# A kernel's own scheduler: dates for the next pair's x operands, and a smaller margin for pressing work

## The chip, the cores and the metric

One core of one Trainium2 chip runs the whole program: TensorE (PE), VectorE (DVE), ScalarE (ACT), GpSimd (POOL) and SyncE (SP), which issues nearly all transfers. The metric is the device time of one execution in microseconds (us). Before the change the median of three runs is 1017.37 us (1017.28 to 1018.18).

## The reference

Attention with a sigmoid in place of the softmax, and then two MLPs one behind the other, all in float32:

```python
scores = scale * np.matmul(q, k.transpose(0, 1, 3, 2)) - np.log(S)     # (4, 12, 448, 448)
attn = 1.0 / (1.0 + np.exp(-scores))
x = np.matmul(attn, v)                     # heads side by side: (1792, 768)
h = x @ w_in;  r = np.maximum(h, 0.0)      # first MLP, 768 -> 2048 -> 768
x = (r * r) @ w_out
h = x @ w_in2                              # second MLP, same sizes
out = (np.maximum(h, 0.0) + alpha * np.minimum(h, 0.0)) @ w_out2
```

The weights arrive as float64.

## The kernel before, in words

Every float32 product is made from a rounded "high" part and the rest, the "low" part: three matmuls (high by high, high by low, low by high) in place of one. ACT makes high parts (an activation that copies into the rounded type), DVE or POOL make low parts (a subtraction). The inner products of the MLPs are also made by a scheme of seven block products from sums and differences of blocks (Strassen's kind), so an x operand or a weight operand is often a sum of blocks before it is split.

The attention comes first (about 159 us, written out in a fixed order, untouched here). After it come 32 units of work, `UNITS` in line 164: layer (2) by pair of batches (2) by eight blocks of two 128-wide slices of the hidden width. Eight units of one layer and one pair are called a phase: phase 0 is layer 0, pair 0; phase 1 is layer 0, pair 1; phase 2 is layer 1, pair 0; phase 3 is layer 1, pair 1. A unit n belongs to phase n // 8. In phases 0 and 2 each unit does its inner products (line 555) and its outer products (line 578), and its weights are made on the spot: a load of 64-bit words into the buffer `raw` (lines 197 to 205), two ACT passes (`scale`, lines 216 and 218), a DVE pass that joins the words (line 231), sums (lines 252 to 258), and the split (lines 269 and 273). The buffer `raw` has two halves, and the load of the next unit's inner weights takes both, so it waits until the outer weights in it have been joined. In phases 1 and 3 the weights come back from DRAM (lines 714 and 890), and the outer products are made for two units at a time (`out_block`, lines 872 to 1031, matmuls in line 942, sums in line 905, splits in lines 919 to 934).

Inside a unit the result of an inner product leaves its PSUM bank by an ACT copy (line 762) or a DVE addition (line 766), then goes through the nonlinearity (lines 732 to 748) and a split (lines 736 and 749) to the outer products; their results are added up by DVE (lines 840 and 973).

**The x operands of the next pair.** While one phase runs, the x operands for the next phase are prepared: `add_x_sum` (line 641) adds a difference of two blocks (line 295), `add_waiting` (line 1039) adds an ACT copy into the one buffer `stage` (line 299), a subtraction into its other half (line 302) and a store of `stage` to DRAM by SP (line 1043). In phase 1 the blocks are loaded in pieces from DRAM (`add_pieces`, line 1048). POOL does differences and subtractions in phases 0 and 1, DVE in phase 2 (`X_BY`, line 1036). Lines 1085 to 1100 hand these steps out to units: four to a unit in phases 0 and 2, from the second unit on, five to a unit in phase 1. At the end of a phase the stored operands are loaded into the x buffers (line 1107). There is one `stage`, so a step's copy waits for the store of the step before it.

**What sets the order.** From line 609 on nothing is issued at once: `Plan.add` records every step with its engine, a cost in us and what it reads and writes. `Plan.run` (lines 50 to 127) then plays the whole list through and issues the steps in the order of the times that come out. TensorE's steps keep their order; each has a due time, the sum of PE costs before it. Any other step is due so early that what needs it can be in time (line 65); `due` is the latest start. In `choose` an engine takes, of the steps that are ready, the one due first, whatever unit it was added in, and it leaves a step aside if a step due earlier would become ready before that one ends and its end would come later than that due time less `MARGIN` (line 96). A step that is not left aside runs as soon as its engine is free, however far off its due time is. The order on each engine, SP's queue of transfers among them, is then fixed when the program runs.

Of the kernel before, what the change touches and what calls it, by code (L numbers as in the profile page):

```python
# [9 lines left out]
F32 = mybir.dt.float32  # L10
# [9 lines left out]
class Plan:  # L20
# [5 lines left out]


    HOP = 0.10
    MARGIN = 2.5
    DEPTH = 3.0  # L30
    AFTER_OWN = {"ACT": 0.12, "POOL": 0.05}
    TAIL = {"PE": 0.17, "DVE": 0.085, "ACT": 0.095, "POOL": 0.04}

    def __init__(self):
        self.jobs, self.last, self.readers = [], {}, {}

    def add(self, engine, us, emit, reads=(), writes=(), port=False, size=0):
        reads, writes = set(reads), set(writes)
        before = {self.last[k] for k in reads | writes if k in self.last}
        for k in writes:  # L40
            before |= self.readers.pop(k, set())
        me = len(self.jobs)
        before.discard(me)
        self.jobs.append((engine, us, emit, before, port, size))
        for k in writes:
            self.last[k] = me
        for k in reads:
            self.readers.setdefault(k, set()).add(me)

    def run(self):  # L50
        jobs, n = self.jobs, len(self.jobs)
        after = [[] for _ in jobs]
        for j, job in enumerate(jobs):
            for i in job[3]:
                after[i].append(j)

        def length(j):
            return jobs[j][1] if jobs[j][0] != "SP" else jobs[j][5] + 2.0

        at, due, pe = 0.0, [0.0] * n, [j for j in range(n) if jobs[j][0] == "PE"]  # L60
        for j in pe:
            due[j] = at
            at += jobs[j][1]
        for j in reversed(range(n)):
            late = min((due[s] - self.HOP for s in after[j]), default=at + 50.0) - length(j) - self.TAIL.get(jobs[j][0], 0.0)
            due[j] = min(due[j], late) if jobs[j][0] == "PE" else late
        left = [len(job[3]) for job in jobs]
        ready = [0.0] * n
        engines = ("PE", "DVE", "ACT", "POOL", "SP", "NIL")
        free = dict.fromkeys(engines, 0.0)  # L70
        waiting = {e: [] for e in engines}
        next_pe = 0
        port_free = dma_free = 0.0
        for j in range(n):
            if not left[j]:
                waiting[jobs[j][0]].append(j)
        order = []

        def begin(j, t):
            t = max(t, ready[j])  # L80
            if jobs[j][0] == "SP":
                t = max(t, dma_free - self.DEPTH)
            return max(t, port_free) if jobs[j][4] else t

        def choose(e, give_way=True):
            queue = waiting[e]
            if e == "PE":
                queue = [j for j in queue if j == pe[next_pe]]
            if not queue:
                return None  # L90
            t = max(free[e], min(begin(j, free[e]) for j in queue))
            now = sorted((j for j in queue if begin(j, free[e]) <= t + 1e-9), key=lambda j: due[j])
            soon = [j for j in queue if begin(j, free[e]) > t + 1e-9]
            for j in now:
                end = t + jobs[j][1]
                if any(due[s] < due[j] and begin(s, free[e]) < end and end > due[s] - self.MARGIN for s in soon):
                    continue
                if e == "POOL" and give_way and any(jobs[s][4] and due[s] < min(due[j], end) and max(free["DVE"], ready[s]) < end for s in waiting["DVE"]):
                    continue
                return t, j  # L100
            if not soon:
                return None
            s = min(soon, key=lambda j: begin(j, free[e]))
            return begin(s, free[e]), s

        while len(order) < n:
            t, j, e = min([(*c, e) for e in engines if (c := choose(e))] or [(*c, e) for e in engines if (c := choose(e, False))])
            engine, us, emit, before, port, size = jobs[j]
            waiting[e].remove(j)
            if e == "PE":  # L110
                next_pe += 1
            free[e] = t + us
            end = t + us + self.TAIL.get(e, 0.0)
            if port:
                port_free = t + us
            if e == "SP" or size:
                dma_free = max(dma_free, t + 0.1) + size
                end = dma_free + 2.0
            order.append((t, j))
            for s in after[j]:  # L120
                left[s] -= 1
                ready[s] = max(ready[s], t + us + self.AFTER_OWN.get(e, 0.0) if jobs[s][0] == e and e != "SP" else end + self.HOP)
                if not left[s]:
                    waiting[jobs[s][0]].append(s)
        self.span = free["PE"]
        for t, j in sorted(order):
            jobs[j][2]()
# [3 lines left out]
def fused_kernel(ctx: ExitStack, tc: tile.TileContext, q, k, v, w1i, w1o, w2i, w2o, alpha, out):  # L131
# [15 lines left out]
    nc = tc.nc  # L147
    B, H, S, D = q.shape
# [144 lines left out]
    def x_sum(p, i, c, eng):  # L293
        to, x, y = (x_block(p, name, c) for name in X_SUM[i])
        eng.tensor_sub(to, x, y)  # L295
# [11 lines left out]
    with tc.manual_schedule():  # L307
# [6 lines left out]
        with tc.tile_pool(name="apool", bufs=1) as apool, tc.tile_pool(name="apsum", bufs=1, space=bass.MemoryType.PSUM) as psum:  # L314
# [145 lines left out]
            for what in X_ORDER[:-1]:  # L460
                i = int(what[1])
# [6 lines left out]
            for d in range(ND):  # L468
                u, w = 2 * d, 2 * d + 1
                i = d - 4  # L470
# [64 lines left out]
        stage = mpool.tile([P, 2, S], F32R, name="stage")  # L535
# [73 lines left out]
        plan = Plan()  # L609
        add = plan.add  # L610
# [11 lines left out]
        def dve(cols):  # L622
            return 0.07 + 0.00105 * cols

        def pool(cols):
            return 0.13 + 0.0023 * cols

        PE_IN, PE_OUT = 0.2027, {384: 0.1740, 512: 0.2270}
        BYTES = 4 * P

        def moved(size, run):

            return size / run * (0.037 + run / 30e3) / 16

        def cells_of(p, name, c):
            kh, t = PLACE[name]
            if p is None:
                return old_cells(PIECES + (kh * 2 + t) * S, S)
            return [("acc", p, ((kh * KH + c) * 2 + t) * S // CELL + k) for k in range(S // CELL)]

        def add_x_sum(p, i, c, engine):
            to, x, y = X_SUM[i]
            add(engine, pool(S) if engine == "POOL" else dve(S), lambda: x_sum(p, i, c, nc.gpsimd if engine == "POOL" else nc.vector), cells_of(p, x, c) + cells_of(p, y, c), cells_of(p, to, c), port=True)

        def add_x_parts(p, i, c, engine, where, keys):
            hi, lo = where
# [71 lines left out]
        def old_cells(at, size):  # L718
            return [("acc", 0, k) for k in range(at // CELL, -(-(at + size) // CELL))]
# [316 lines left out]
        X_BY = ("POOL", "POOL", "DVE")  # L1036
        x_kept = {}

        def add_waiting(n, i, c, p, engine):
            keys = [("stage", 0), ("stage", 1)]  # L1040
            add_x_parts(p, i, c, engine, (stage[:, 0], stage[:, 1]), keys)
            to = x_kept[n // NB]
            add("SP", 0.05, lambda: nc.sync.dma_start(out=to[i][:, :, c], in_=stage.bitcast(F32)), keys, [("x_kept", i, c)], size=moved(2 * S * BYTES, 4 * S))

        def add_pieces(c):

# [3 lines left out]
        for n in range(NU):  # L1050
            layer, p, fp = UNITS[n]
            other, phase = 1 - p, n // NB
            by_pieces = phase == 1
# [31 lines left out]
            if phase < 3:  # L1085
                if fp == 0:
                    x_kept[phase] = [dpool.tile([P, 2, KH, S], F32, name=f"kept_x{n}_{i}") for i in range(7 if by_pieces else 4)]
                    if by_pieces:
                        steps = [(what, c) for c in range(KH) for what in ("load", *X_ORDER) if c < KH - 1 or what not in ("p3", "p4", "p5", "p6")]
                    else:  # L1090
                        steps = [None] * 4 + [(what, c) for what in X_WAITING if what != "p3" or layer == 0 for c in range(KH)]
                if fp < NB - 1:
                    each = 5 if by_pieces else 4
                    for what, c in filter(None, steps[each * fp:each * fp + each]):
                        if what == "load":
                            add_pieces(c)
                        elif what[0] == "s":
                            add_x_sum(None if by_pieces else other, int(what[1]), c, X_BY[phase])
                        else:
                            add_waiting(n, int(what[1]), c, None if by_pieces else other, X_BY[phase])  # L1100
            outward = add_outward(n) if p == 0 else None
# [8 lines left out]
            if p == 0:  # L1110
                next(outward, None)
            elif fp % 2:
                next(part_way, None)
            else:
                part_way = out_block(n + 1)
                next(part_way)
        plan.run()


# [28 lines left out]
```

## Time and profile before

| | us |
|---|---|
| median of the runs (three) | 1017.37 |
| the profiled execution | 1018.92 |
| its span | 1017.1 |
| PE busy | 1008.2 (99%) |
| DVE busy | 730.2 (72%) |
| ACT busy | 636.6 (63%) |
| POOL busy | 281.0 (28%) |

The span is the profiled execution from its first to its last instruction. TensorE's granted clock is 1.00 in all stretches. "Busy" of PE contains matmuls that run into each other; idle time of the other engines costs only where PE waits. The rows further down come from the page's list of engines, from tables by stretch (time, busy time and instructions of each engine, granted clock, DMA share, GB/s), from lists of instructions in order of time (start, duration, engine, line, operation, result and inputs, count; in brackets idle time before it and what ended it), and from the chain of work that ended last.

### The profile page before, as it was taken

The numbers are of one execution on the slowest core, as the hardware profiler recorded it, in microseconds if no ns is written. First come the engines' busy times: TensorE is split into PE (matmuls) and PEld (weight loads), VectorE is DVE, ScalarE is ACT, GpSimd is POOL, SyncE is SP. The second block draws the span as 40 slices with busy tenths as digits, with TensorE's granted clock in tenths as the row PEclk, the third lists the DMA queues.
The fourth block names the chain that finished last, engine by engine and source line by source line (L and its number), as shares of the span: only waits on it lengthen the run. The fifth ranks groups of instructions, "written<-read, shape, count | busy, mean of one in ns | idle before, by whom it ended". The sixth has DMA issues, their size and how long they took to land.

```text
span 1017.1 us, 15048 instructions
## 1 busy us (share of the span) xinstructions
PE 1008.2 (99%) x5539; PEld 886.6 (87%) x5539; DVE 730.2 (72%) x968; ACT 636.6 (63%) x976; POOL 281.0 (28%) x240
## 2 busy tenths in 40 slices
PE   9999999999999999999999999999999999999998
PEld 6555557988998899998899999999999999999998
DVE  5556886367777774868786885888888776676857
ACT  4566777767776655776566667666666565535352
POOL 0001222346321130435342511111111227070703
PEclk9999999999999999999999999999999999999999
DMA  6566747677776699698768966766666983626133
GB/s 145 148 175 166 201 118 291 268 285 281 280 279 231 246 418 364 224 335 292 279 247 330 372 240 217 251 251 245 217 229 234 391 282 83 198 80 201 45 95 109
DMA packets 133337, 237.59 MB, mean 234 GB/s; under 512 B 56976, under 2 KB 81552, under 8 KB 131856
## 3 DMA queue, kind: packets, MB, share of 16 engines
q1 hardware_dynamic: 130384, 234.79, 67.3%
q10 hardware_dynamic: 2880, 1.84, 0.6%
q8 instruction: 44, 0.72, 0.3%
q14 instruction: 29, 0.24, 0.1%
HBM read 150.74 MB, written 85.85 MB: 233 GB/s over the span
## 4 chain that ended last, share of the span: by engine, by line
PE 90%; DVE 4%; DMA 2%; issue 2%; POOL 1%; ACT 1%; SPq 0%; DVEq 0%; POOLq 0%; ACTq 0%
PE h L555 38%; PE o L578 20%; PE o L942 11%; PE h L942 7%; PE av L408 5%; PE sc L388 4%; PE h L578 1%; DMA raw<-in_moe_w_in_dram 1%; PE scr L398 1%; PE tp L355 1%; PE av L416 1%; DMA words<-kept5o 1%; PE tp L358 1%; DVE flat L361 1%; PE busy L432 0%
## 5 line engine op out<-in xcount | busy, mean ns | idle before, releaser
L555 PE MATMUL h<-x,wi 128*128 128x448 f32 (+1 forms) x2064 | 416.4, 361 | 1.6 <-DVE c L766 1.6
L555 PEld LDWEIGHTS h<-x,wi 128*128 128x128 f32 x2064 | 379.6, 188 | 31.7 <-DVE c L766 2.0
L700 POOL TENSOR_TENSOR wo<-words,wo 128x384 fp32r<-128x384 f32 x64 | 69.3, 1107 | 242.9 <-ACT wo L703 238.8
L578 PE MATMUL o<-g,wo 128*128 128x512 f32 (+1 forms) x528 | 112.9, 367 | 1.0 <-DVE acc L840 0.8
L578 PE MATMUL o<-wo,g 128*128 128x384 f32 x624 | 112.4, 335 | 0.0
L578 PEld LDWEIGHTS o<-wo,g 128*128 128x128 f32 x624 | 109.1, 188 | 0.4
L578 PEld LDWEIGHTS o<-g,wo 128*128 128x128 f32 x528 | 96.0, 188 | 14.2 <-DVE acc L840 2.4
L840 DVE TENSOR_TENSOR acc<-o,acc 128x768 f32<-128x768 f32 (+2 forms) x91 | 85.6, 950 | 12.9 <-PE o L578 12.7
L766 DVE TENSOR_TENSOR c<-h,c 128x448 f32<-128x448 f32 x72 | 44.6, 622 | 69.2 <-PE h L555 66.9
L390 ACT ACTIVATE a<-sc,bias 128x896 f32<-128x896 f32 x72 | 69.1, 1004 | 35.6 <-PE av L408 22.6
L924 POOL TENSOR_TENSOR wo<-acc,wo 128x384 fp32r<-128x384 f32 x30 | 35.7, 1209 | 137.2 <-ACT wo L919 137.2
L216 ACT ACTIVATE raw<-raw 128x768 f32<-128x768 f32 x64 | 58.2, 909 | 23.3 <-DMA raw<-in_moe_w_out_dram 19.3
L762 ACT ACTIVATE c<-h 128x448 f32<-128x448 f32 x72 | 38.7, 539 | 43.9 <-PE h L555 43.8
L749 DVE TENSOR_TENSOR g<-c,g 128x448 fp32r<-128x448 f32 x64 | 43.4, 681 | 31.6 <-ACT c L737 21.5
L302 POOL TENSOR_TENSOR stage<-acc,stage 128x448 fp32r<-128x448 f32 x29 | 35.9, 1237 | 99.2 <-ACT stage L299 99.2
L231 DVE SCALAR_TENSOR_TENSOR words<-raw 128x768 int32<-128x768 int32 x53 | 52.8, 1005 | 9.7 <-ACT raw L218 8.9
L408 PE MATMUL av<-a,v 128*64 128x448 f32 x288 | 59.4, 548 | 0.0
L218 ACT ACTIVATE raw<-raw 128x768 int32<-128x768 uint32 x64 | 57.7, 902 | 0.0
L973 DVE TENSOR_TENSOR acc<-o,acc 128x384 f32<-128x384 f32 (+1 forms) x84 | 46.1, 580 | 14.7 <-PE o L942 14.4
L295 POOL TENSOR_TENSOR acc<-acc 128x448 f32<-128x448 f32 x28 | 40.6, 1451 | 27.9 <-DMA acc<-late 16.2
L745 DVE SCALAR_TENSOR_TENSOR c<-c,nal,pos 128x448 f32<-128x448 f32 x48 | 34.5, 718 | 17.0 <-ACT c L744 15.9
L408 PEld LDWEIGHTS av<-a,v 128*64 128x64 f32 x288 | 18.5, 136 | 28.7 <-issue 26.8
(168 smaller groups left out, 1691.2 us busy)
## 6 DMA issues: line engine op xcount, KB each, us to landing
wi<-kept_w SPq DMA_DIRECT2D x112, 384.0 KB, 5.2
kept_w<-wi SPq DMA_DIRECT2D x45, 768.0 KB, 4.3
raw<-in_moe_w_out_dram SPq DMA_DIRECT2D x32, 768.0 KB, 4.8
raw<-in_moe_w_in_dram SPq DMA_DIRECT2D x13, 1536.0 KB, 8.9
kept_x<-stage SPq DMA_DIRECT2D x38, 448.0 KB, 5.8
x<-kept_x SPq DMA_DIRECT2D x10, 1344.0 KB, 11.0
kept_w<-wi SPq DMA_DIRECT2D x22, 384.0 KB, 4.9
v<-in_v_dram SPq DMA_DIRECT2D x24, 192.0 KB, 2.9
```

What stands on the lines that cost most here:

```text
L216: nc.scalar.activation(half.bitcast(F32), half.bitcast(F32), AF.Prelu, scale=2.0 ** -112, alpha=2.0 ** 32)
L218: nc.scalar.activation(half, half.bitcast(U32), AF.Copy, scale=2.0 ** -29 * (1 - 2.0 ** -12), bias=-0.5 + 7.5 * 2.0 ** -12)
L231: nc.vector.scalar_tensor_tensor(out=to, in0=raw_words(at, 1, both), scalar=3, in1=raw_words(at, 0, both), op0=ALU.logical_shift_left, op1 ...
L390: nc.scalar.activation(sig[u, j], ps[:, :, :S], AF.Sigmoid, bias=bias[:, :1], scale=SCALE)
L408: nc.tensor.matmul(avs[u][h * D:(h + 1) * D, :S], vals[u][:, h, j, :], a[:, h, :], start=(u % 2 == 0 and j == 0), stop=(u % 2 == 1 and j = ...
L555: nc.tensor.matmul(ps[:, a:e], W[:, OPERAND[k], wp, c * P:(c + 1) * P], X[k][:, xp, c, a:e], start=(k in OPENING and c == 0 and i == 0 and ...
L578: nc.tensor.matmul(ps, *ops, start=(begin and i == 0), stop=(end and i == len(ways) - 1), skip_group_check=True)
L700: nc.gpsimd.tensor_sub(WO[j][:, 1, at], words["o"][:, j, at], WO[j][:, 0, at])
L766: add("DVE", dve(S), lambda: nc.vector.tensor_add(to, hb[b][:, :S], to), [("h", b), *key], key)
L840: add("DVE", dve(count), lambda dst=dst, src=src: nc.vector.tensor_add(dst, src, dst), [*src_keys, *cells], cells)
L942: nc.tensor.matmul(ps[:, a:e], stationary(ways, j), moving(ways, j)[:, a:e], start=(start and j == 0 and i == 0 and a == 0), stop=(j == 1 ...
L973: add("DVE", dve(out_wide), lambda: nc.vector.tensor_add(part, src, part), [key, *cells], cells)
```

## The change

`MARGIN` goes from 2.5 to 1.0. `Plan` gets a list of the places where units end (`step`), and a step may be given `by`, a unit's number. Where a step has one, its due time is at most the due time of the first PE step that was added after that unit, less the step's own length; steps that it depends on are dated back from there as before. The x differences, and the stores of `stage`, that are handed out in unit n get `by` = n + 2. Costs, instructions and their dependencies are as before; only the order of issue can differ.

```diff
-    MARGIN = 2.5
+    MARGIN = 1.0
...
-    def add(self, engine, us, emit, reads=(), writes=(), port=False, size=0):
+        self.steps, self.by = [], {}
+    def step(self):
+        self.steps.append(len(self.jobs))
+    def add(self, engine, us, emit, reads=(), writes=(), port=False, size=0, by=None):
...
+        if by is not None:
+            self.by[me] = by
...
             due[j] = min(due[j], late) if jobs[j][0] == "PE" else late
+            if j in self.by and self.by[j] < len(self.steps):
+                due[j] = min(due[j], next((due[i] for i in pe if i >= self.steps[self.by[j]]), at) - length(j))
...
-        def add_x_sum(p, i, c, engine):
+        def add_x_sum(p, i, c, engine, by):
...
-            add(engine, pool(S) if engine == "POOL" else dve(S), lambda: x_sum(p, i, c, nc.gpsimd if engine == "POOL" else nc.vector), cells_of(p, x, c) + cells_of(p, y, c), cells_of(p, to, c), port=True)
+            add(engine, pool(S) if engine == "POOL" else dve(S), lambda: x_sum(p, i, c, nc.gpsimd if engine == "POOL" else nc.vector), cells_of(p, x, c) + cells_of(p, y, c), cells_of(p, to, c), port=True, by=by)
...
-            add("SP", 0.05, lambda: nc.sync.dma_start(out=to[i][:, :, c], in_=stage.bitcast(F32)), keys, [("x_kept", i, c)], size=moved(2 * S * BYTES, 4 * S))
+            add("SP", 0.05, lambda: nc.sync.dma_start(out=to[i][:, :, c], in_=stage.bitcast(F32)), keys, [("x_kept", i, c)], size=moved(2 * S * BYTES, 4 * S), by=n + 2)
...
-                            add_x_sum(None if by_pieces else other, int(what[1]), c, X_BY[phase])
+                            add_x_sum(None if by_pieces else other, int(what[1]), c, X_BY[phase], n + 2)
...
                 next(part_way)
+            plan.step()
         plan.run()
...

```

## Rows read from the trace of the kernel before

**Rows 1.** The page's list of engines: busy us, share of the span, instructions.
```profile
PE 1008.2 (99%) x5539; PEld 886.6 (87%) x5539; DVE 730.2 (72%) x968; ACT 636.6 (63%) x976; POOL 281.0 (28%) x240
```

**Rows 2.** Stretches: us; PE, PEld, DVE, ACT, POOL busy (instructions); clock, DMA share, GB/s.
```profile
158.94:379.78 220.84, 219.81 (x1098) 199.33 (x1097) 151.53 (x196) 152.37 (x244) 69.36 (x59) 1.00 0.79 292
213.85:241.97 28.12, 27.86 (x138) 24.81 (x137) 18.94 (x24) 17.39 (x29) 16.10 (x14) 1.00 0.68 232
269.26:296.54 27.28, 27.28 (x138) 24.95 (x137) 20.30 (x27) 19.99 (x32) 7.77 (x7) 1.00 0.80 289
296.54:324.90 28.36, 27.59 (x138) 24.87 (x137) 19.66 (x27) 18.44 (x29) 3.99 (x4) 1.00 0.71 252
...
379.78:587.97 208.19, 206.18 (x1046) 190.33 (x1044) 153.09 (x184) 134.11 (x208) 77.12 (x62) 1.00 0.85 307
...
483.20:536.67 53.47, 51.84 (x263) 47.45 (x261) 41.08 (x50) 30.99 (x49) 22.02 (x18) 1.00 0.72 259
536.67:587.97 51.30, 51.30 (x263) 47.66 (x261) 40.23 (x53) 34.43 (x53) 17.90 (x15) 1.00 0.95 360
587.97:807.15 219.18, 219.18 (x1193) 212.04 (x1192) 178.68 (x258) 141.89 (x230) 38.86 (x35) 1.00 0.68 248
```

**Rows 3.** Instructions in order of time, sixth unit of phase 0.
```profile
299.46 0.90 ACT L218 ACTIVATE raw<-raw 128x768 int32<-128x768 uint32 x1
...
302.30 0.62 DVE L766 TENSOR_TENSOR c<-h,c 128x448 f32<-128x448 f32 x1 [1.60 <-PE h L555]
302.84 1.56 DVE L231 SCALAR_TENSOR_TENSOR words<-raw 128x768 int32<-128x768 int32 x1
...
304.49 0.38 SPq L205 DMA_DIRECT2D raw<-in_moe_w_in_dram  x1
...
305.10 0.62 DVE L749 TENSOR_TENSOR g<-c,g 128x448 fp32r<-128x448 f32 x1 [0.69 <-ACT c L737]
...
307.31 2.15 PEld L578 LDWEIGHTS o<-g,wo 128*128 128x128 f32 x12
```

**Rows 4.** The chain that ended last, same unit: start, us, what.
```profile
304.49 10.74 DMA raw<-in_moe_w_in_dram
```

**Rows 5.** Instructions in order of time, third unit of phase 0.
```profile
226.03 0.62 DVE L749 TENSOR_TENSOR g<-c,g 128x448 fp32r<-128x448 f32 x1 [0.40 <-ACT c L737]
...
230.29 2.99 POOL L295 TENSOR_TENSOR acc<-acc 128x448 f32<-128x448 f32 x2
...
230.89 1.37 DVE L273 TENSOR_TENSOR wi<-words,wi 128x768 fp32r<-128x768 f32 x1
...
232.18 2.12 DVE L749 TENSOR_TENSOR g<-c,g 128x448 fp32r<-128x448 f32 x2
```

**Rows 6.** Instructions in order of time, third unit of phase 2.
```profile
642.76 11.12 PE L555 MATMUL h<-x,wi 128*128 128x224 f32 x55
...
649.28 0.62 DVE L766 TENSOR_TENSOR c<-h,c 128x448 f32<-128x448 f32 x1
...
652.48 0.63 DVE L749 TENSOR_TENSOR g<-c,g 128x448 fp32r<-128x448 f32 x1
...
653.52 2.15 PEld L578 LDWEIGHTS o<-wo,g 128*128 128x128 f32 x12
```

**Rows 7.** Instructions in order of time, phase 1, around its longest PE wait.
```profile
473.89 0.60 SPq L1043 DMA_DIRECT2D kept_x<-stage  x1
...
494.16 0.95 DVE L231 SCALAR_TENSOR_TENSOR raw<-raw 128x768 int32<-128x768 int32 x1
```

**Rows 8.** The chain that ended last, same stretch: start, us, what.
```profile
475.25 8.09 DMA words<-kept5o
```

**Rows 9.** The store of `stage` in phase 0, and in phase 1: durations, first and last start.
```profile
L1043 SPq DMA_DIRECT2D kept_x<-stage x12: 518/519/1059, 185.3 to 292.9; - x12
...
L1043 SPq DMA_DIRECT2D kept_x<-stage x17: 513/519/604, 425.1 to 571.7; - x17
```

**Rows 10.** Waits in phase 1: us in total, times, longest.
```profile
ACT stage L299 <- DMA kept_x<-stage: 14.9, 7, 4.2
```

## What is forecast, and from which rows

> **What bounds the kernel now.** I read the page's list of engines first: PE is busy 1008.2 of 1017.1 us [rows 1], so nothing but PE's own work and the short waits in it sets the end. Then the table by stretch, where the reader is to compare length and PE busy time [rows 2]. Phase 2 has no gap at all: 219.18 of 219.18. An undisturbed unit of phase 0 takes 27.28 (269.26 to 296.54), so phase 0's 220.84 holds 220.84 - 8 x 27.28 = 2.60 of delay; two units have most of it, 28.12 (0.84 over) and 28.36 (1.08 over). An undisturbed pair of units of phase 1 takes 51.30 (536.67 to 587.97), so phase 1's 208.19 holds 208.19 - 4 x 51.30 = 2.99, of which the pair from 483.20 has 53.47 - 51.30 = 2.17. An order of issue adds or removes no PE work, so 2.60 + 2.99 = 5.6 us is all that it can win (0.55% of the time). Third, the lists in order of time and the chain, for what stands behind each delay.
>
> **The smaller margin.** It removes no instruction. It lets DVE, ACT and POOL begin a filler step (a join, a scale, a sum) beside a pressing one that would become ready before it ends, as long as 1.0 us, not 2.5, is left to the pressing one's latest start.
>
> *The sixth unit of phase 0 (1.08).* ACT ends the last scale at 299.46 + 0.90 = 300.36, and the join that needs it could run on DVE then. DVE stands idle for 1.60 us, does the pressing addition at 302.30 and only then the join, at 302.84 [rows 3]. The load of the next inner weights needs that join and is issued at 304.49; it lands 10.74 us later and is at the head of the chain that delays PE [rows 3, 4]. How much room had the addition? Its chain to the split takes 305.10 + 0.62 - 302.30 = 3.42, PE loads the result as weights at 307.31 [rows 3], so its latest start is 307.31 - 3.42 = 303.89, 1.59 after it could start. A margin of 2.5 is more than that room, so no filler may overlap its start at all; a margin of 1.0 leaves 0.59 for overlap. The join alone takes 0.95 (a twin, [rows 7]) and on the real times would have fitted before 302.30; on the planner's, which differ, it must have been ready later, less than 0.95 before the addition, to be left aside. If it runs at 300.4 the load goes out some 2.4 us earlier, more than the 1.08 lost. Bounds: nothing gained (the planner took the join for not ready yet, for its time and the chip's differ) to 1.08. I take 1.08, since the idle time stands exactly where the rule applies.
>
> *The third unit (0.84).* Here two POOL differences (2.99 for two) run beside DVE's split (1.37) and the two subtractions that PE waits for (2.12 for two, where one alone takes 0.62) [rows 5]: 2.12 - 2 x 0.62 = 0.88 of slowing, the whole 0.84. The margin doesn't see it; a new order may part them or not. Bounds 0 to 0.84, taken half: 0.42. Of the 0.68 in the other six units I take 0.2.
>
> *Phases 2 and 3.* Nothing to win in phase 2. What could be lost? The addition at 649.28 could have started at 642.76 + (302.30 - 296.54) = 648.52 [rows 2, 3, 6]; from 649.28 its chain ends at 652.48 + 0.63 = 653.11, PE loads the result at 653.52, 0.41 later [rows 6]. So its latest start is 649.69, the room 1.17, of which the new margin opens 1.17 - 1.0 = 0.17. That is less than the 0.41 still free: cost 0, at most 8 units x (1.5 - 0.41) = 8.7 if the margin were all that held DVE back. Phase 3 has the same forms and no x steps: 0.
>
> *What it gives back.* In phases 0 and 1 pressing steps start up to 0.59 later by the sum above; where this meets one of the slowed instructions PE waits. No row shows such a wait; bounds 0 and 0.84 (the one delay of that kind) in each of the 4 units with POOL differences in phase 0 and of the 4 pairs in phase 1, 6.7 in all. I take 0.3, near the low end, since 1.0 of room stays and the slowing of one subtraction is 0.44.
>
> One rule of the Trainium skill speaks against the change here: "SBUF — State Buffer", section Who interferes with whom, has a DVE instruction with two SBUF inputs and a GpSimd instruction that reads SBUF exclude each other for a whole instruction. By it one meeting could cost a pressing DVE step all of a POOL difference, by [rows 5] some 1.2 to 1.5, more than the margin of 1.0, so the cost would be nearer to one delay for each meeting; the trace shows 0.44 for one subtraction, which the sum goes by. It makes the third rival below more likely, and is its mechanism.
>
> **The dates.** A step gets a date only to be ranked by; it never waits for it. In phase 0 the twelve stores go out from 185.3 to 292.9 [rows 9]; the first group's new date is the start of the fifth unit, 269.26, and the last must be in time for 379.78 in either version [rows 2]. They run 80 us ahead of both: the order changes by next to nothing, 0. Phase 2 is the same. In phase 1 it can bite. The seventeen stores go out from 425.1 to 571.7 [rows 9], (571.7 - 425.1) / 16 = 9.2 apart. Counted back from the end of the phase, the first would be due some 80 us before 588 (an estimate: 17 x about 5, the planner's own lengths of copy, subtraction and store); by the new date, the start of the fourth unit of the phase, some 445. So x steps now outrank out-product weight work that is due between. Every one of them moves its copy (ACT), its subtraction and its differences (POOL), its load of pieces and its store (SP, 0.60 each at 473.89 [rows 7]) up the queues; behind them wait the weight loads of the same SP queue and the weight splits on ACT and POOL. But they can't move far: ACT waits seven times, 14.9 us in all, for the store of the step before to free `stage` [rows 10].
>
> The longest delay, 2.17, has a late weight load at its head: 8.09 us for `words` issued at 475.25, after the store at 473.89 [rows 7, 8]; then DVE still does joins for phase 2 (0.95 at 494.16 [rows 7]) before the addition that PE waits for. If x steps sit some us earlier, the loads no longer crowd there and the 2.17 goes; if they crowd elsewhere, another such delay comes. Bounds: a gain of 2.99 to a loss of 2.17. I take a gain of 1.0, a third of what is there, for dates and margin together.
>
> **The sum.** 1.08 + 0.42 + 0.2 + 1.0 - 0.3 = 2.4 us. The profiled execution took 1018.92 (span 1017.1 and 1.8 around it), 1.55 above the median of the runs: 1018.92 - 2.4 = 1016.5, less 1.55 gives 1015.0 for a median.
>
> **Rivals.**
> - *Nothing measurable (within 0.2%, 2.0 us, which is about what measurement tells from no change).* The two large delays begin with transfers of 10.74 and 8.09 [rows 4, 8], which an order hardly shortens, and the dates bind in one phase only. For it: `stage` is bound by its own store [rows 10]. Against it: the 1.60 of idle DVE in front of a ready join [rows 3]. Only the third unit's 0.42 and some of the rest is won: 1017.37 - 0.7 = 1016.7. That the dates do nothing at all belongs here.
> - *Everything is won.* Of 5.6 some 5 goes: 1012.3. For it: each delay is one wait at one place. Against: half of phase 0's comes from POOL beside DVE [rows 5], which stays.
> - *Slower.* POOL's x steps meet pressing DVE work with too little room: the third unit's 0.84 [rows 2, 5] comes again wherever POOL differences run, four units of phase 0 and four pairs of phase 1. Five of eight: 1017.37 + 5 x 0.84 = 1021.6, if nothing is won. It decides from three such delays on with nothing won (2.5 us, beyond 2.0), from six on if 2.4 is won. For it: the x steps rank higher in phase 1, where POOL is busiest (77.12 us [rows 2]). Against: only one unit of eight in phase 0 shows it now, with x steps in four of them.
>
> **Chances.** Forecast 0.38 (its own range 1013.5 to 1015.3: from 1.08 + 0.84 + 2.0 won to just beyond what can be measured), everything won 0.07, nothing measurable 0.36, slower 0.19. So faster by over 0.2% 0.45, within 0.36, slower 0.19. The range from 1012.4 to 1019.8 leaves out about 0.03 below and the larger slower cases, 0.14, above.
>
> **What would show it.** In the trace after: the join in the sixth unit of phase 0 ahead of the addition, the load of line 205 issued some 2 us earlier there, unit lengths near 27.3 in phase 0; the phase's first store near 185 as before. In phase 1 the pair at 483 shorter than 53.47, stores not much closer than 9 us. Phases 2 and 3 as long as before to 0.2. I am wrong if phase 2 grows, if PE waits behind DVE's splits or additions come up in units that had none, or if the sixth unit keeps its 28.36 with the join early.

## The result, and the profile after

The changed kernel takes 1032.53 us (median of four runs, 1029.63 to 1034.42); the kernel before took 1017.33 beside it. The ratio is 1.0141, 95% interval 1.0125 to 1.0157: 1.4% slower, where 0.2% faster was forecast, and outside the range. The profiled execution is the fastest of the four, 1029.63 with a span of 1027.8, so the profile explains 10.7 of the 15 us (before: 1018.92 and 1017.1). The lines named here stand ten lower in the changed kernel (L555 is L565, L766 is L776, L269 is L279, L216 is L226).

The page's list of engines of the changed kernel (busy us, share of the span, instructions):

```profile
PE 1012.5 (99%) x5539; PEld 884.8 (86%) x5539; DVE 734.4 (71%) x968; ACT 632.9 (62%) x976; POOL 293.1 (29%) x240
```

Its table by stretch (us; PE, PEld, DVE, ACT, POOL busy; clock, DMA share, GB/s): phases 0, 1 and 2, then the third unit of phase 0, the pair of phase 1 from 482.79, and one unit of phase 2.

```profile
158.66:379.97 221.31, 219.42 (x1099) 199.39 (x1097) 154.12 (x196) 150.88 (x243) 71.36 (x59) 1.00 0.79 295
379.97:589.07 209.10, 206.35 (x1045) 190.42 (x1044) 155.51 (x186) 132.23 (x207) 83.47 (x62) 1.00 0.85 304
589.07:817.87 228.80, 224.16 (x1194) 210.74 (x1193) 176.83 (x256) 141.94 (x233) 43.51 (x37) 1.00 0.66 238
213.52:242.88 29.36, 27.82 (x138) 24.80 (x137) 20.22 (x24) 19.70 (x33) 15.18 (x12) 1.00 0.64 236
482.79:537.84 55.05, 52.38 (x263) 47.44 (x261) 42.98 (x50) 32.25 (x50) 26.46 (x18) 1.00 0.79 278
728.53:758.21 29.68, 28.55 (x150) 26.14 (x150) 22.58 (x32) 18.00 (x30) 4.83 (x4) 1.00 0.63 220
```

Against [rows 2]: phase 2 grows by 9.62 us (219.18 to 228.80), phase 1 by 0.91, phase 0 by 0.47; the first three pairs of phase 3 take 154.77 against 154.78. Instructions and clock are as before. So in these two executions nearly all of it is in phase 2, the phase without a gap (more traces of the same orders put more into phases 0 and 1, see below). Its eight units took 27.4 each; after, they take 27.41, 27.40, 27.40, 27.97, 29.28, 29.68, 29.99 and 29.67: the loss begins with the fourth and repeats.

What is different there? Instructions in order of time on ACT in one such unit after (start, us, line, result and inputs; in brackets the idle time before it and what ended it):

```profile
744.89 0.92 ACT L226 ACTIVATE raw<-raw 128x768 f32<-128x768 f32 x1 [0.53 <-DMA raw<-in_moe_w_in_dram]
745.71 0.89 ACT L228 ACTIVATE raw<-raw 128x768 int32<-128x768 uint32 x1
746.49 0.53 ACT L753 ACTIVATE pos<-h 128x448 f32<-128x448 f32 x1
746.91 0.54 ACT L754 ACTIVATE c<-h 128x448 f32<-128x448 f32 x1
...
754.37 0.85 ACT L279 ACTIVATE wi<-sums_anew 128x768 fp32r<-128x768 f32 x1 [1.96 <-DVE sums_anew L264]
757.32 0.90 ACT L226 ACTIVATE raw<-raw 128x768 f32<-128x768 f32 x1 [2.11 <-DMA raw<-in_moe_w_out_dram]
758.12 0.89 ACT L228 ACTIVATE raw<-raw 128x768 int32<-128x768 uint32 x1
758.89 0.85 ACT L279 ACTIVATE wi<-sums_anew 128x768 fp32r<-128x768 f32 x1
```

and the same work of the kernel before, in its third unit of phase 2:

```profile
657.97 0.53 ACT L743 ACTIVATE pos<-h 128x448 f32<-128x448 f32 x1
658.40 0.54 ACT L744 ACTIVATE c<-h 128x448 f32<-128x448 f32 x1
658.82 0.92 ACT L216 ACTIVATE raw<-raw 128x768 f32<-128x768 f32 x1
...
668.08 0.92 ACT L216 ACTIVATE raw<-raw 128x768 f32<-128x768 f32 x1 [1.61 <-DMA raw<-in_moe_w_out_dram]
668.89 0.84 ACT L269 ACTIVATE wi<-sums_anew 128x768 fp32r<-128x768 f32 x1
669.62 0.91 ACT L218 ACTIVATE raw<-raw 128x768 int32<-128x768 uint32 x1
```

Two places have changed. *First place:* the two scales (L226, L228) of the next unit's first inner words now stand ahead of the two copies (L753, L754) that take the last hidden block out of PSUM, not behind them; the first of them waits there for its load (0.53 by the transfer). *Second place:* the second scale of the outer words now stands ahead of the last inner weight split (L279), not behind it. In the list of the whole phase this order comes in five units after, the third to the seventh; the loss shows in as many, the fourth to the eighth, each behind one that has the order.

The chain that ended last shows what comes of it (start, us, what; after, sixth unit of phase 2):

```profile
728.98 0.88 ACT raw L228
729.85 0.74 ACT wi L279
...
731.50 1.77 DVE wi L283
733.26 1.73 DVE acc L850 x2
734.99 0.88 DVE words L241
...
735.89 8.98 DMA raw<-in_moe_w_in_dram
...
744.89 0.92 ACT raw L226
```

Before, the chain of this stretch is PE alone. After, it is a loop of the queues: the scale goes ahead of the split, the split on ACT and DVE comes later for it, then the join that frees the buffer `raw`, so the next load of the inner weights is issued later, lands later (8.98), and holds up ACT in the next unit, where the scales now stand in front of the copies. What of this the order does alone, without late loads, the experiments below tell. PE's own waits in phase 2 are short (the longest 0.65) but add up to the 4.6 us by which 228.80 exceeds its busy 224.16; the rest of the loss lies in matmuls that count as busy from the first to the last of a run (224.16 against 219.18 for the same matmuls).

### The profile page after: what moved, and what is told of

The parts are those of the page before. It is cut to its first block, busy times and chain, and to the rows that moved or that the text cites. A ratio compares the mean times of both kernels' runs of the same rounds, so it can differ in the third digit from the quotient of the medians.

```text
span 1027.8 us, 15036 instructions
## 1 busy us (share of the span) xinstructions
PE 1012.5 (99%) x5539; PEld 884.8 (86%) x5539; DVE 734.4 (71%) x968; ACT 632.9 (62%) x976; POOL 293.1 (29%) x240
## 4 chain that ended last, share of the span: by engine, by line
PE 75%; DVE 10%; DMA 7%; ACT 5%; issue 2%; SPq 0%; ACTq 0%; DVEq 0%
PE h L565 29%; PE o L588 15%; PE o L952 11%; PE h L952 6%; PE av L418 5%; PE sc L398 4%; DMA raw<-in_moe_w_in_dram 4%; DVE acc L850 3%; DVE words L241 2%; DMA raw<-in_moe_w_out_dram 1%; DVE wi L283 1%; ACT raw L228 1%; ACT raw L226 1%; PE scr L408 1%; DVE g L759 1%
## 5 line engine op out<-in xcount | busy, mean ns | idle before, releaser
L565 PE MATMUL h<-x,wi 128*128 128x448 f32 (+1 forms) x2064 | 419.5, 362 | 4.3 <-ACT c L772 2.7
L565 PEld LDWEIGHTS h<-x,wi 128*128 128x128 f32 x2064 | 378.9, 188 | 38.2 <-ACT c L772 5.2
L588 PE MATMUL o<-wo,g 128*128 128x384 f32 x624 | 114.5, 337 | 2.3 <-DVE g L759 1.3
L776 DVE TENSOR_TENSOR c<-h,c 128x448 f32<-128x448 f32 x72 | 44.7, 622 | 68.2 <-PE h L565 66.5
L934 POOL TENSOR_TENSOR wo<-acc,wo 128x384 fp32r<-128x384 f32 x30 | 39.3, 1330 | 137.2 <-ACT wo L929 130.4
L226 ACT ACTIVATE raw<-raw 128x768 f32<-128x768 f32 x64 | 58.0, 906 | 31.4 <-DMA raw<-in_moe_w_out_dram 24.4
L312 POOL TENSOR_TENSOR stage<-acc,stage 128x448 fp32r<-128x448 f32 x29 | 38.4, 1324 | 111.5 <-ACT stage L309 99.0
L241 DVE SCALAR_TENSOR_TENSOR words<-raw 128x768 int32<-128x768 int32 x53 | 56.5, 1069 | 14.7 <-ACT raw L228 13.3
L228 ACT ACTIVATE raw<-raw 128x768 int32<-128x768 uint32 x64 | 57.7, 901 | 0.0
L755 DVE SCALAR_TENSOR_TENSOR c<-c,nal,pos 128x448 f32<-128x448 f32 x48 | 33.6, 699 | 16.4 <-ACT c L754 15.2
L418 PEld LDWEIGHTS av<-a,v 128*64 128x64 f32 x288 | 18.5, 136 | 28.7 <-issue 26.7
```

The costliest lines, as they stand in the source:

```text
L226: nc.scalar.activation(half.bitcast(F32), half.bitcast(F32), AF.Prelu, scale=2.0 ** -112, alpha=2.0 ** 32)
L228: nc.scalar.activation(half, half.bitcast(U32), AF.Copy, scale=2.0 ** -29 * (1 - 2.0 ** -12), bias=-0.5 + 7.5 * 2.0 ** -12)
L241: nc.vector.scalar_tensor_tensor(out=to, in0=raw_words(at, 1, both), scalar=3, in1=raw_words(at, 0, both), op0=ALU.logical_shift_left, op1 ...
L418: nc.tensor.matmul(avs[u][h * D:(h + 1) * D, :S], vals[u][:, h, j, :], a[:, h, :], start=(u % 2 == 0 and j == 0), stop=(u % 2 == 1 and j = ...
L565: nc.tensor.matmul(ps[:, a:e], W[:, OPERAND[k], wp, c * P:(c + 1) * P], X[k][:, xp, c, a:e], start=(k in OPENING and c == 0 and i == 0 and ...
L588: nc.tensor.matmul(ps, *ops, start=(begin and i == 0), stop=(end and i == len(ways) - 1), skip_group_check=True)
```

## The experiments

Theories that stood against each other when they began: **A**, the margin does it, by ACT's order in phase 2; **A1**, in detail: the planner takes the inner load as landed earlier than it is, so that a filler let in ahead of pressing work waits for a transfer (a plan that knew would lose nothing); **A2**, against A1: that order costs whatever the transfers do; **B**, the dates do it. All kernels are edits of the changed one where nothing else is said. Every time is a median, every ratio is to the kernel before run beside it.

**Each half alone.** `dates_only`:

```diff
-    MARGIN = 1.0
+    MARGIN = 2.5
```

> MARGIN back at 2.5, the dates kept. Theory A (the smaller margin alone costs the 15 us, through the order on ACT in phase 2): within 2 us of before, 1015 to 1019.5, phase 2 at 219.2 and only phase 1 different, by up to 2 us either way. Rival B (the dates push x steps of POOL and DVE in front of pressing work): 1025 or more, with phase 2 above 225.

Measured: 1023.9 us, ratio 1.006 (1.0038 to 1.0082), between the two forecasts. `margin_only`:

```diff
-        if by is not None:
+        if False:
```

> MARGIN 1.0, no dates. Theory A: 1028 to 1034 like the changed kernel, phase 2 again near 228. Rival B: 1015 to 1020, phase 2 near 219.

Measured: 1033.41, ratio 1.0152 (1.0135 to 1.0169): as slow as both together. The dates alone cost less, at another place: in phase 2 only the first unit is long (31.45); the next six take 27.40 to 27.44 and the last 28.22. Beside the small margin the dates add nothing.

**Which engine's margin.** `wide_act` keeps 2.5 for ACT, `narrow_act` gives 1.0 to ACT only:

```diff
-   ... end > due[s] - self.MARGIN for s in soon):
+   ... end > due[s] - (2.5 if e == "ACT" else self.MARGIN) for s in soon):      # wide_act
+   ... end > due[s] - (1.0 if e == "ACT" else 2.5) for s in soon):              # narrow_act
```

> The changed kernel with 2.5 of margin for steps on ACT alone; DVE and POOL keep 1.0. Theory A: nearly all comes back, 1016 to 1021, phase 2 at 219 to 222. Rival B, or a margin that matters on DVE: 1027 or more.

> The changed kernel with 1.0 of margin for steps on ACT alone; DVE and POOL have 2.5. Theory A: still slow, 1026 to 1034. A margin that matters on DVE: 1016 to 1020.

Measured: `wide_act` 1019.02, ratio 1.0009 (0.9999 to 1.002), no difference; `narrow_act` 1026.56, ratio 1.0089 (1.0064 to 1.0113), with units of phase 2 from the fourth on of 28.1 to 29.3. The table by stretch of `wide_act`, phase 2:

```profile
586.18:805.53 219.35, 219.35 (x1193) 212.10 (x1192) 179.80 (x258) 142.00 (x230) 41.69 (x37) 1.00 0.67 245
```

PE busy is again the whole length. ACT's margin is what loses phase 2. (Two early units of `wide_act` have both scales ahead of the copies too, and PE waits for nothing there: the place alone does not cost in every unit. What decides it was not tested.) The same with the dates taken out, `wide_act_nodates` (both edits above):

> No dates, 1.0 of margin on DVE and POOL, 2.5 on ACT. By the order on ACT as cause: phase 2 at 219 to 221; phases 0 and 1 as before within 2 us, so 1016 to 1020. If it needs the dates to be good at the border: first unit of phase 2 above 28.

Measured: 1020.22, ratio 1.0019 (1.0006 to 1.0032): no gain hidden in the smaller margin of DVE and POOL, which a cleaned-up ACT would have shown.

**One place of ACT's queue at a time.** In the kernel before (margin 2.5, no dates) the finished order is changed by hand: `move_last` makes the second change of place (seven units of phase 2), `move_first` the first one (six units), `move_both` both.

```diff
+        for n in range(17, 24):      # move_last, move_both
+            plan.moves.append((("scale", n, "o", 1, 0), "before", ("high", n, "s34")))
+        for n in range(17, 23):      # move_first, move_both
+            for word in (1, 0):
+                plan.moves.append((("scale", n + 1, "i", 0, word), "before", ("pos", n, 0, 0)))
```

> The kernel before, with the second scale of the outer words put ahead of the last split of the inner weights in units 17 to 23, as the changed kernel has it. If this place alone starts the chain: phase 2 at 223 to 229, the whole 4 to 10 us over before. If it needs the other place: phase 2 at 219 to 221, the whole within 2 us of before.

> The kernel before, with the scales of the next unit's first inner words ahead of the two copies of the last hidden block in units 17 to 22. If this place alone holds PE up (the copies wait for a late load): phase 2 at 223 to 229. If it needs the other: 219 to 221, within 2 us of before.

> The kernel before with both moves. If the two places on ACT explain the loss: phase 2 at 225 to 230 and the whole 6 to 11 us over before. If the order of DVE in the changed kernel is needed too: phase 2 below 223.

Measured: 1028.25 (ratio 1.0106, 1.0074 to 1.0139), 1026.55 (1.0077, 1.0058 to 1.0097) and 1036.23 (1.0176, 1.0146 to 1.0205). Phase 2 is 9.3, 8.8 and 17.8 longer than the 219.18 of before: the two places add up, though both together cost more than was forecast (17.8 for at most 11). `move_last` has six long units (28.84 to 29.03, 9.3 / 6 = 1.5 over 27.4 each), `move_first` five (28.91 to 29.21, 1.5 to 1.8 over) and two slightly longer ones, `move_both` six (29.47 to 30.56). PE's waits in phase 2 of `move_last` (engine and line waited for: us in total, times, longest) name an ACT copy out of PSUM that stands behind the delayed split in ACT's queue:

```profile
PE h L573 <- ACT c L784: 7.2, 6, 1.4
```

In `move_first` the chain of phase 2 runs over ACT and DVE, here in its fifth unit:

```profile
716.57 0.78 ACT raw L236
717.35 0.42 ACT pos L765
717.77 0.44 ACT c L766
...
718.23 0.69 DVE c L767
```

No transfer is in this chain from 660 to 800 us, nor in that of `move_last`: the order on ACT costs without a load in the chain. That speaks for A2.

So either place alone, with nothing else of the change, makes the loss. The changed kernel has both and loses less, 9.6 in five units: its DVE order was planned along with ACT's, and the next kernel shows that the two orders hang together.

**Both places put back by hand in the changed kernel**, `after_moved` (the first change of place is undone by moving the copies, the second by moving the scale):

```diff
+            plan.moves.append((("scale", n, "o", 1, 0), "behind", ("high", n, "s34")))
...
+                plan.moves.append(((sign, n, 0, 0), "before", ("scale", n + 1, "i", 0, 1)))
```

> The changed kernel, in which two places of ACT's order in phase 2 alone are put back by hand as they were before: the second scale of the outer words goes behind the last split of the inner weights (units 17 to 23), and the two copies of the last hidden block go ahead of the scales of the next unit's first words (17 to 22). If these two places are the cause (A2: in-order ACT, chain from a transfer over a scale to a weight split to PE): phase 2 at 219 to 222, the whole at 1021 to 1025. If the rest of the order (DVE, the others) matters as much: phase 2 above 225, the whole above 1027.

Measured: 1033.83, ratio 1.0152 (1.0129 to 1.0175): a miss, nothing comes back. From the third to the seventh its units are 29.26 to 29.27, one like the other. The chain in one of them:

```profile
748.63 0.43 ACT c L769
749.07 0.79 ACT raw L237
749.86 0.79 ACT raw L239
...
750.68 0.96 DVE words L252
751.63 0.60 DVE c L770
```

There is no transfer in it any more. ACT does copies, then scales, as before (only one split of `g` still stands behind both scales, not between them, and it is not in this chain); but DVE's queue, planned for the other order, still has the join (`words`) ahead of the step (`c` L770) on which PE's next work hangs, and this join waits for the second scale. Putting ACT's order back without that of DVE gains nothing here.

**Is it the transfers?** Three kernels for A1. `late_land` lets the planner take every transfer as 2.5 us longer; `late_wide` does that with the margin of 2.5; `short_load` leaves the plan as it is and loads only a third of the rows of both inner weight slices in layer 1 (two thirds of each load are left out).

```diff
-                end = dma_free + 2.0
+                end = dma_free + 4.5                                   # late_land, late_wide
...
+        some = NC // 3 if layer else NC                                # short_load
+        nc.sync.dma_start(out=d[:, :some], in_=(w1i, w2i)[layer][:some * P, ...
```

> The changed kernel, whose planner takes a transfer to land 4.5 us after its last byte is moved, not 2.0 (readiness only; due times and margin as changed). Theory A1 (with 1.0 the planner puts steps that wait for a transfer in front of pressing ones on ACT, and the transfers land later than it reckons): most comes back, 1016 to 1022, phase 2 at 219 to 223, and fewer ACT waits for transfers. Theory A2 (1.0 is too little for ACT whatever the transfers do): 1027 or more.

> MARGIN 2.5 with the dates, and the planner's landing at 4.5 us. Against the run with 2.5 and dates alone (1023.9, first unit of phase 2 at 31.45 for 27.40): by A1 the late store in front of a pressing weight copy there is planned round, the unit is back under 28.5 and the whole at 1014 to 1019. If the dates cost by themselves (x steps too high in rank): 1022 or more.

> The changed kernel, with a third of each load of both inner weight slices in layer 1 (the rest is left out, so results of layer 1 are from old words). Same order of issue; only the load lands earlier, by some 4 of its 9 us. Theory A1 and its loop (load, scale, join, second load, scale, join, next load is longer than a unit of phase 2): phase 2 at 219 to 223, the whole at 1019 to 1025. Theory A2: phase 2 stays above 226, the whole at 1029 or more.

Measured: `late_land` 1035.37 (1.0174, 1.0159 to 1.0189), `late_wide` 1040.02 (1.022, 1.0202 to 1.0237): misses as totals, since the first unit of phase 2 takes 41.4 and 41.8 (see below). Behind it, though, six units of `late_land` are at 27.40 with the margin of 1.0, as A1 has it (the last takes 28.26); in ACT's list neither of the two places is taken from the fourth unit on. `short_load` 1028.21 (1.0107, 1.0084 to 1.0129), between its two forecasts: its loads land in 6.0 us at the median (8.8 after), its long units take 27.9, 28.3, 28.5, 28.5 and 29.6. The four of 29.28 to 29.99 have become 28.26 to 29.59, on average 28.7 for 29.7: the excess over 27.4 falls from 2.3 to 1.3. Its chain in phase 2:

```profile
757.59 0.44 ACT raw L229
758.03 0.73 ACT wi L280
...
759.66 1.77 DVE wi L284
761.43 1.73 DVE acc L851 x2
```

The load is out of the chain, the scale ahead of the split is still in it. A1 is part of the truth: in the changed kernel, whose chain has three such loads (8.98 to 9.86 us), the later landing adds 1.0 a unit to the 1.3 that are left when the load is out of the chain.

**A margin for the scales alone**, `wide_scales`, 2.5 for the two scale steps and 1.0 for all else:

```diff
-   ... end > due[s] - self.MARGIN for s in soon):
+   ... end > due[s] - (2.5 if j in self.scales else self.MARGIN) for s in soon):
```

> The changed kernel, 2.5 of margin for the two ACT scales of the raw words alone, 1.0 for all else. If the scales are what must be held back (A1): 1016 to 1021, phase 2 at 219 to 222. If other ACT fillers matter as much: 1025 or more.

Measured: 1030.05, ratio 1.0119 (1.0104 to 1.0134), the total of the second forecast but not for its reason. From the fourth unit on neither place is taken in ACT's list, and the units from the second to the sixth are back at 27.40; but the first of phase 2 takes 35.15 and the last 30.85, in which PE waits 1.4 for DVE's split of `g`: one loss traded for others.

**The other loss: the border before phase 2.** `dates_in_1` keeps the dates in phase 1 only, with the margin of 2.5; `margin_200` and `margin_400` have no dates and margins of 2.0 and 4.0.

```diff
+    ... by=n + 2 if n // NB == 1 else None)               # dates_in_1, MARGIN = 2.5
+    MARGIN = 2.0                                         # margin_200, if False: in add
+    MARGIN = 4.0                                         # margin_400, if False: in add
```

> MARGIN 2.5, dates for the steps of phase 1 alone (the dates of phases 0 and 2 change next to nothing in the order). If the dates cost by what they move in phase 1 (the last x step and its load end too near the next phase): like the run with all dates, 1021 to 1026, the first unit of phase 2 near 31. If the dates of phase 2 pull its first x step over the border: first unit near 27.4, 1015 to 1020.

> No dates, MARGIN 2.0. In phase 2 it puts the first scale of the next words, not the second, ahead of the last hidden copies in units 19 to 22; the outer words' scales keep their place. If each scale that passes costs by itself: phase 2 at 221 to 225, 2 to 6 us over before. If the room of 2.0 is enough: 219 to 220 and 1016 to 1019.5.

> No dates, MARGIN 4.0. If more room is what PE needs wherever it waits: 1012 to 1016. If 2.5 already holds all back that matters and more only leaves engines idle: 1017 to 1025, with the first unit of phase 2 longer because the x steps of phase 1 end later.

Measured: `dates_in_1` 1023.87 (1.0049, 1.003 to 1.0068): the cost of the dates comes from phase 1. `margin_200` 1018.89 (1.0003, 0.999 to 1.0015): no difference; the units 19 to 22 do not have the order that I expected: against before, a scale has moved ahead of the copies in one early unit only. `margin_400` 1040.48 (1.0211, 1.019 to 1.0233), slower than both forecasts. The instructions in order of time in `margin_400`, SP's queue and PE at the border:

```profile
602.47 0.32 SPq L1117 DMA_DIRECT2D x<-kept_x  x1
...
612.05 7.13 PE L565 MATMUL h<-x,wi 128*128 128x448 f32 x27 [18.45 <-DMA x<-kept_x]
```

PE waits 18.45 us for the last of the next pair's x operands. The time at which that last load is issued sorts the kernels by the length of the first unit of phase 2 (before and after, the phase begins at 588 and 589, in the others at 585 to 591). In `wide_scales`, `late_land`, `late_wide` and `margin_400` PE waits for this load itself (3.98, 6.91, 5.14 and 18.45 us); for the rest the table shows only that the two go together. Only `wide_act_nodates` stands outside, with 28.69 for a load at 572.2:

| last load of x issued, us | first unit of phase 2, us |
|---|---|
| after 569.6, `wide_act` 571.7, before 577.7 | 27.4 |
| `margin_only` 582.3 | 28.04 |
| `narrow_act` 583.0 | 29.39 |
| `dates_in_1` 584.3 | 29.92 |
| `dates_only` 585.3 | 31.45 |
| `wide_scales` 590.8 | 35.15 |
| `late_land` 597.3 | 41.40 |
| `late_wide` 600.9 | 41.80 |
| `margin_400` 602.5 | 49.18 |

In `dates_only` the load itself is not waited for. The same view of ACT and PE there:

```profile
585.38 0.58 ACT L309 ACTIVATE stage<-acc 128x448 fp32r<-128x448 f32 x1 [5.28 <-DMA kept_x<-stage]
585.87 0.83 ACT L279 ACTIVATE wi<-sums_anew 128x768 fp32r<-128x768 f32 x1
...
588.90 0.67 PE L565 MATMUL h<-x,wi 128*128 128x448 f32 x2 [0.89 <-ACT wi L279]
590.64 10.55 PE L565 MATMUL h<-x,wi 128*128 128x448 f32 x43 [1.08 <-DVE wi L283]
```

and the last of these rows in `dates_in_1`:

```profile
592.57 9.00 PE L565 MATMUL h<-x,wi 128*128 128x448 f32 x43 [0.87 <-DVE wi L283]
```

In `dates_only` ACT stands idle 5.28 us in front of a copy into `stage`, until the store of the step before is done, and behind that copy in its queue is the split of phase 2's first weights. So the x steps are late by the chain through the one `stage`, and what stands behind them on ACT is late too. Why the dates, which only pull steps forward in the ranking, push the last of them back stays open: no run took the dates of single steps away. The seventeen stores of phase 1 run from 422.9 to 578.4 us in `dates_only` and from 425.1 to 571.7 before [rows 9]: they begin earlier and end later.

Part of these lengths is TensorE's clock. The table by stretch of `dates_only`, right behind the waits above:

```profile
592.00:595.00 3.00, 3.00 (x10) 2.67 (x10) 0.00 (x0) 0.54 (x1) 3.00 (x4) 0.53 1.01 419
```

The granted clock of 0.53 is close to the lower of its two levels (1.2 of 2.4 GHz). The 43 matmuls there take 10.55 us. In `dates_in_1`, with waits nearly the same (1.08 and 0.87) and a clock of 1.00, they take 9.00. The difference is 1.55 of the 4.05 that the unit is over. In `margin_400` the clock of this unit is 0.79, and PE is busy 30.72 for 27.39.

## Why the prediction was wrong

**The step that failed** is "*Phases 2 and 3.* Nothing to win in phase 2 ... cost 0, at most 8 units x (1.5 - 0.41) = 8.7 if the margin were all that held DVE back". The phase cost 9.62, more than that bound. It priced the room of one DVE addition [rows 6] and took that for the place where the margin acts. The margin acts on every engine at every pair of a filler and a pressing step; the two places that it opened were on ACT, two scales of 0.9 in front of the copies and one in front of a split. I had read no ACT row of phase 2. And the cost isn't the length of the filler: one scale of 0.9 costs 1.5 a unit in `move_last`, two of 0.9 cost 1.5 to 1.8 together in `move_first`. By the chains this is because behind ACT come DVE's split, the additions and the join, and then the next load, each in its queue's order.

**"I am wrong if phase 2 grows, if PE waits behind DVE's splits or additions come up in units that had none"** came true in both parts.

**The sixth unit (1.08).** The order changed as forecast, but it was not what the delay hung on. Instructions in order of time after:

```profile
301.18 1.64 DVE L241 SCALAR_TENSOR_TENSOR words<-raw 128x768 int32<-128x768 int32 x1
302.85 0.38 SPq L215 DMA_DIRECT2D raw<-in_moe_w_in_dram  x1
303.21 0.62 DVE L776 TENSOR_TENSOR c<-h,c 128x448 f32<-128x448 f32 x1 [0.39 <-PE h L565]
```

The join has gone ahead of the addition, and the load goes out 302.85 - 297.45 = 5.40 after the unit's start, 7.95 before [rows 2, 3]: 2.5 earlier, 2.4 was put. Yet the unit takes 27.94, so only 0.42 of the 1.08 came. And the 1.08 was no debt of the order at all: `dates_only` has before's own order in phase 0,

```profile
301.43 0.62 DVE L776 TENSOR_TENSOR c<-h,c 128x448 f32<-128x448 f32 x1 [1.36 <-PE h L565]
301.97 1.54 DVE L241 SCALAR_TENSOR_TENSOR words<-raw 128x768 int32<-128x768 int32 x1
```

with nearly the same idle time before the addition and the load 7.92 after the unit's start, and its sixth unit took 27.28; the load landed in 9.2 there. `move_last`, `move_first` and `move_both`, which have before's order in phases 0 and 1 too, took 27.29 to 27.31. One profiled execution was read as the rule: its load landed late at 10.74 [rows 4].

**The third unit (0.42 won)** went the other way, 28.12 to 29.36. In order of time after:

```profile
232.43 1.27 POOL L312 TENSOR_TENSOR stage<-acc,stage 128x448 fp32r<-128x448 f32 x1 [2.48 <-ACT stage L309]
...
232.61 3.07 DVE L759 TENSOR_TENSOR g<-c,g 128x448 fp32r<-128x448 f32 x2
...
233.78 2.93 POOL L305 TENSOR_TENSOR acc<-acc 128x448 f32<-128x448 f32 x2
```

Two subtractions of 0.62 took 3.07 beside POOL, (3.07 - 1.24) / 2 = 0.92 more each, not the 0.44 of [rows 5]. This is the slower rival's mechanism, in one unit, not five. It comes each time: the unit takes 29.36 to 29.45 in the three traces with this order in phases 0 and 1 (after, `after_moved`, `short_load`), and 28.12 to 29.04 in the five with before's. The rule cited for it, the Trainium skill's "SBUF — State Buffer", section Who interferes with whom, makes the shared port pair an exclusive lock. Held for a whole POOL instruction it could cost up to 1.27 or 2.93 / 2 = 1.47 by these rows (an estimate); the 0.92 lies below that and at twice the 0.44 that the sum went by.

**Phase 1 (1.0 won)** lost 0.91; the pair that had 53.47 has 55.05. Late loads still stand at its head (7.36 for `raw` at 487.06 in the chain). The 2.17 of this pair were in part one execution's too: with before's order the other traces have 51.8 to 53.0, with the new one 54.8 and 56.0. **The 0.3 given back** was too little: phases 0 and 1 lost 1.4 net in the two profiled executions, most of it in the third unit and this pair, and some 3.7 by more traces (below).

**The dates.** That they change next to nothing in phases 0 and 2 and bite in phase 1 only was right: alone, they leave the order of every engine in phase 0 as it was, and `dates_in_1` costs what `dates_only` does. That they would win there was wrong: 1023.9 against 1018.2 beside it. The rival "slower" named the sign, but its mechanism, POOL's x steps, is not in phase 2 at all, where DVE does them; of its meetings the rows above show the third unit's alone.

**Where the rest of the 15 us is.** The two profiled executions differ by 10.7 only: that of before took longer than its median (1018.92 for 1017.37), that of after is the fastest of four. Other traces with the same orders in phases 0 and 1 show more. With before's order these two phases take 429.03 (before), 426.61 (`move_last`), 428.41 (`move_first`) and 427.07 us (`move_both`), 427.8 on average; with the new order 430.41 (after), 432.06 (`after_moved`) and 432.13 (`short_load`), 431.5 on average. So some 3.7 is lost there, not 1.4, and with the 9.62 of phase 2 that makes 13.3 of 15.2. With ACT's margin back at 2.5 the two phases take 427.87 (`wide_act`, one trace). The last 2 us stay open: no slower execution of the changed kernel was traced.

## What to carry to other kernels

A list scheduler's margin isn't a waste where no wait shows: in a phase where PE never waits there is nothing to win and everything to lose, so list for every in-order queue which fillers the new margin would let pass which pressing steps, fillers that wait for a transfer among them, and price each place through all that stands behind it. A constant such as this one has two cliffs (here the loss in phase 2 at 1.0 and the late x operands at 4.0, with 2.0 and 2.5 alike between), and a profile taken at one value shows neither. Before a short delay in one execution is counted as winnable, see whether it comes in a second one of the same order.

## What the runs showed of the hardware

One ACT instruction of 0.9 us put ahead of its neighbour cost 1.5 us in each of six units of 27.4 (`move_last`), two of 0.9 ahead of two copies cost 1.5 to 1.8 in each of five (`move_first`), and the two changes added up (9.3, 8.8, and 17.8 together). With the same order on every engine phase 0 took 220.84 us in one execution and 219.29 in another (the kernel before and `dates_only`), by 1.08 less in the sixth unit alone. Two DVE subtractions beside POOL work took 2.11 to 2.12 in one order (five traces) and 3.07 in another (three). After two PE waits of about 1 us each the granted clock fell to 0.53 for a stretch in one execution (`dates_only`) and stayed at 1.00 in another (`dates_in_1`).
